# Attention and two gated MLPs on one core: Newton steps of two batches' roots moved to plain products, a gated tile kept in SBUF, planner constants set anew

## The chip, the cores and the metric

The kernel runs on one core of one Trainium2 chip. The metric is the device time in microseconds (us) of one execution. The engines are named as in the profile: PE is the matmul engine (PEld its weight loads), DVE the vector engine, ACT the scalar engine, POOL GpSimd, SP the engine whose queue issues most DMAs. Each engine runs its own instructions in order and waits on semaphores of the others.

## The reference, cut to what matters

Four batches, 12 heads, 448 positions, head size 64. Attention with root-mean-square normalised q and k feeds two gated MLPs in a row:

```python
rms = np.sqrt(np.mean(x * x, axis=-1, keepdims=True) + 1e-06)
q_n, k_n = q / rms_q * g_q, k / rms_k * g_k
attn = softmax(q_n @ k_n.T / 8);  x = attn @ v            # -> (4, 448, 768)
h = np.maximum(x @ moe_w_in, 0.0)                          # 768 -> 1024
x = (h * sigmoid(conv3(h))) @ moe_w_out                    # 1024 -> 768
out = (sigmoid(conv5(x)) * (x @ moe2_w_val)) @ moe2_w_out  # 768 -> 768
```

Inputs arrive as 64-bit floats; weights are converted on the chip and every operand is split into a high and a low fp16 part, so that a product is three fp16 matmuls.

## The kernel before, in words

**Stages.** A batch's attention is 21 units (three groups of four heads, seven units each: six of 128 query rows and one of remainders). A unit is: the score matmuls into a PSUM pair (`qk`), row maxima on DVE (`smax`, one `TENSOR_REDUCE ps<-ps 128x2` and a small product that goes to the tile `mx`), two exponentials on ACT (`sexp`), the split into fp16 parts `p`, a DMA transpose to `pt`, and the matmuls with the values (`av`). A batch's MLP has four stages, called w_in (8 tiles), w_out (6), w_val (6) and the output (7 half tiles). The attention of batch b+1 runs beside the MLP of batch b; the output of batch 0 is done late, after the w_in stage of batch 1. The MLP of batch 3 has nothing beside it.

**Roots.** Before a group of heads starts, `prep` squares and sums q and k and calls `rroot(x, y, t)`: an add, a shift and an integer step give a first guess of 1/sqrt(x), then three Newton steps refine it. `x` is the tile `ssq`, `y` one of three tiles `root`, `t` the tile `half`, 128 rows by 30 columns. A Newton step is three DVE instructions: `half<-root`, `half<-half,ssq`, `root<-half,root`, so nine in a root. The normalisation of k (`kin<-kin,root` on POOL) and the row maxima wait for it. There are twelve groups; the first is solved in three pieces.

**Gated tile.** In a w_in tile (`w_in_tile`) ACT writes relu(h) back into the PSUM bank `ps` and the middle tap to `scr`; DVE adds the two outer taps (`scr<-ps,cw,scr`); ACT takes tanh; `mul` multiplies into the PSUM bank; `hi` copies the high half to `act`; `lo` subtracts it (`act<-ps,act 128x448`) and closes the bank. `scr` has four buffers.

**Order.** All instructions are recorded with a wish time (`at`) and then put into an order by a planner (class `Plan`): it has estimated costs and picks, engine by engine, the ready instruction of highest priority. An instruction recorded through `vg` or `sub` may go to DVE or POOL, one through `copy` or `times` to DVE or ACT, whichever the planner expects to be done first; a lean (the constants `L_...`) is added to DVE's estimate. The add of log(4096) to `mx` in batches 2 and 3 is such a `vg`. Every instruction of the plan is emitted at line 378, so that is the line in all rows of the profile. What comes out is a fixed order per engine, with buffers and semaphores set at build time.

Of the kernel before, what the change touches and what calls it, by code (L numbers as in the profile page):

```python
# [25 lines left out]
class Plan:  # L26
# [355 lines left out]
def kernel(  # L382
# [172 lines left out]
    W_2 = 70.038  # L555
    W_2_STEP = 3.986
    RS_AT = -1.932
    RS_STEP = -0.224
# [15 lines left out]
    L_SQ = 2.046  # L574
    L_LOAD = 3.479
    L_WHI = 1.477
    L_WLO = 0.815
# [1064 lines left out]
```

## Time and profile before

| | us |
|---|---|
| median of 3 runs (651.45 to 652.5) | 651.65 |
| the profiled execution's own time | 651.15 |
| its span, first to last instruction | 649.4 |
| PE busy | 592.0 |
| DVE busy | 520.7 |
| ACT busy | 419.9 |
| POOL busy | 224.0 |

The shares are of a span with different stages. Attention of batch 0 fills the first 100 us; from there to about 253 us attention of batch 1 runs beside the MLP of batch 0; from about 253 to 420 us attention of batch 2 beside the MLP of batch 1; to about 551 us attention of batch 3 beside the MLP of batch 2; the rest is the MLP of batch 3. The rows below give busy times by these five stretches.

### The profile page before, as it was taken

Reading aid. Unit: us, or ns where it says so; the run is one execution under the profiler, and the core shown is the slowest. Engines: PE = TensorE matmul, PEld = TensorE weight load, DVE = VectorE, ACT = ScalarE, POOL = GpSimd, SP = SyncE. Lnnn points to the kernel's source line nnn. Section 1 sums busy time; section 2 is a strip of 40 time slices with the busy share of each in tenths; the row PEclk is TensorE's granted clock in tenths of the full one; section 3 lists DMA queues with packets and bytes.
Section 4 is the critical chain, followed back from the end, with each engine's and each line's share of the span. In section 5 each row is a group of like instructions: output and inputs, shape, how many; then the busy total and the mean of one; then the engine's idle time right before and its main releaser. Section 6 shows DMA issues by size and latency. Waiting matters only on the chain. (4 is left out here: it accounts for less than half of the span.)

```text
span 649.4 us, 12670 instructions
## 1 busy us (share of the span) xinstructions
PE 592.0 (91%) x4755; PEld 332.0 (51%) x4755; DVE 520.7 (80%) x1059; ACT 419.9 (65%) x735; POOL 224.0 (34%) x246
## 2 busy tenths in 40 slices
PE   4897899897996787999898999999999999999997
PEld 2665586453453344455454555555554565555554
DVE  6989799999999999999678885689997754498720
ACT  4787789878786876698557665578756455272211
POOL 2533465616325624545343442263444101000000
PEclk9988799897997989999999999999999999999999
DMA  8967667985987988993788587884646467200002
GB/s 207 230 141 182 137 127 213 205 204 103 189 165 175 229 169 157 191 204 104 163 165 155 106 141 150 169 166 85 102 90 108 86 124 146 47 0 1 2 13 74
DMA packets 254611, 88.06 MB, mean 136 GB/s; under 512 B 240671, under 2 KB 250453, under 8 KB 254549
## 3 DMA queue, kind: packets, MB, share of 16 engines
q1 hardware_dynamic: 254021, 87.12, 64.2%
q8 instruction: 37, 0.61, 0.4%
q14 instruction: 25, 0.20, 0.1%
q10 hardware_dynamic: 528, 0.13, 0.1%
HBM read 38.59 MB, written 5.51 MB: 68 GB/s over the span
## 5 line engine op out<-in xcount | busy, mean ns | idle before, releaser
L378 PE MATMUL ps<-act,wi 128*128 128x448 f16 x576 | 120.8, 359 | 4.6 <-DVE p L378 1.7
L378 PE MATMUL ps<-act,wo 128*128 128x448 f16 x576 | 122.1, 356 | 2.9 <-DVE act L378 2.6
L378 DVE TENSOR_REDUCE ps<-ps 128x2 f32<-128x896 f32 x84 | 91.2, 1093 | 18.6 <-PE ps L378 18.2
L378 ACT ACTIVATE p<-ps,mx,root 128x448 f32<-128x448 f32 x112 | 75.4, 722 | 41.6 <-POOL mx L378 31.6
L378 PE MATMUL ps<-act,wv 128*128 128x448 f16 x432 | 92.5, 358 | 8.1 <-DVE p L378 4.8
L378 PE MATMUL ps<-w,act 128*128 128x384 f16 (+1 forms) x576 | 93.3, 327 | 1.3 <-ACT osb L378 1.0
L378 PE MATMUL ps<-ka,qa 64*128 64x448 f16 (+3 forms) x560 | 80.9, 384 | 12.7 <-DVE p L378 5.6
L378 PEld LDWEIGHTS <-wi 128*128 128x128 f16 x576 | 55.3, 99 | 59.2 <-issue 14.7
L378 PEld LDWEIGHTS <-wo 128*128 128x128 f16 x576 | 54.9, 99 | 54.6 <-issue 11.2
L378 PE MATMUL ps<-vv,pt 128*128 128x65 f16 (+4 forms) x1488 | 79.8, 202 | 0.0
L378 ACT ACTIVATE act<-ps 128x448 f16<-128x448 f32 (+3 forms) x96 | 50.2, 531 | 44.4 <-PE ps L378 23.2
L378 PEld LDWEIGHTS <-pt 128*128 128x128 f16 (+1 forms) x1512 | 59.8, 101 | 25.3 <-issue 8.9
L378 POOL TENSOR_TENSOR p<-p,p 128x896 f16<-128x896 f32 x28 | 53.4, 1908 | 47.3 <-issue 27.6
L378 PEld LDWEIGHTS <-act 128*128 128x128 f16 (+1 forms) x576 | 48.7, 101 | 35.9 <-issue 8.0
L378 PEld LDWEIGHTS <-wv 128*128 128x128 f16 x432 | 41.1, 99 | 48.7 <-issue 15.2
L378 DVE SCALAR_TENSOR_TENSOR act<-ps,cw,act 128x444 f32<-128x444 f32 (+3 forms) x96 | 63.6, 676 | 0.8
L378 DVE SCALAR_TENSOR_TENSOR w<-w 128x768 uint32<-128x768 uint32 (+1 forms) x56 | 45.8, 826 | 1.6 <-POOL w L378 1.5
L378 PEld LDWEIGHTS <-qa 64*128 64x128 f16 (+1 forms) x528 | 21.8, 97 | 46.9 <-issue 32.7
L378 DVE SCALAR_TENSOR_TENSOR scr<-ps,cw,scr 128x447 f32<-128x447 f32 x64 | 41.8, 675 | 0.5 <-ACT scr L378 0.3
L378 ACT ACTIVATE p<-p 128x896 f16<-128x896 f32 x42 | 39.9, 950 | 0.4
L378 POOL TENSOR_SCALAR mx<-mx 128x2 f32<-128x2 f32 x37 | 9.1, 245 | 87.1 <-DVE mx L378 80.2
L378 POOL TENSOR_TENSOR kin<-kin,gb 112x512 f32<-112x512 f32 x22 | 29.9, 1363 | 17.6 <-ACT tk L378 13.2
(116 smaller groups left out, 920.1 us busy)
## 6 DMA issues: line engine op xcount, KB each, us to landing
w<-in_moe_w_in_dram SPq DMA_DIRECT2D x8, 768.0 KB, 5.2
w<-in_moe_w_out_dram SPq DMA_DIRECT2D x8, 768.0 KB, 5.4
kin<-in_k_dram SPq DMA_DIRECT2D x24, 224.0 KB, 3.6
act<-in_moe_w_out_dram SPq DMA_DIRECT2D x12, 384.0 KB, 4.0
w<-in_moe_w_val_dram SPq DMA_DIRECT2D x12, 384.0 KB, 4.2
out_dram<-osb SPq DMA_DIRECT2D x24, 192.0 KB, 2.2
qin<-in_q_dram SPq DMA_DIRECT2D x35, 128.0 KB, 3.2
vst<-in_v_dram SPq DMA_DIRECT2D x18, 224.0 KB, 3.6
```

What stands on the lines that cost most here:

```text
L378: getattr(getattr(nc, e), method)(*a, **k)
```

## The change

`rroot` gets a flag. With it, a Newton step is four plain instructions instead of three fused ones, each of which may go to DVE or POOL (`L_STEP` is negative, which favours DVE a little). It is set for batches 1 and 2 (`ROOTP_1`, `ROOTP_2`), which have three roots each. `LEAVE_IN` becomes one for batches 2 and 3: `mul` writes the gated tile into `scr`, the PSUM bank is closed there, `hi` reads SBUF and `lo` may go to POOL. A third option (`XSB`) is added and left at zero. About forty constants of the planner change a little.

```diff
     def rroot(x, y, t, pool):
         vg(L_ROOT, "tensor_scalar", x, x, D * 1e-6, None, ALU.add)
...
         for _ in range(3):
+            if pool:
+                vg(L_STEP, "tensor_tensor", t, y, y, ALU.mult)
+                vg(L_STEP, "tensor_tensor", t, t, x, ALU.mult)
+                vg(L_STEP, "tensor_scalar", t, t, -0.5, 1.5, ALU.mult, ALU.add)
+                vg(L_STEP, "tensor_tensor", y, y, t, ALU.mult)
+                continue
             nc.vector.scalar_tensor_tensor(t, y, -0.5, y, ALU.mult, ALU.mult)
             nc.vector.tensor_tensor(t, t, x, ALU.mult)
             nc.vector.scalar_tensor_tensor(y, t, 1.5, y, ALU.add, ALU.mult)
...
-            rroot(ss[:rows, c], rr[:rows, c], tmp[:rows, c])
+            rroot(ss[:rows, c], rr[:rows, c], tmp[:rows, c], ROOT_POOL[b] and not solo)
...
-    LEAVE_IN = (0, 0, 0, 0)
+    LEAVE_0 = 0
+    LEAVE_1 = 0
+    LEAVE_2 = 1
+    LEAVE_3 = 1
+    ROOTP_1 = 1
+    ROOTP_2 = 1
+    L_STEP = -0.143
...
-    L_ROOT = 0.504
+    L_ROOT = 0.445
-    SIGN_VAL = 2
+    SIGN_VAL = 3
-    VLEAD = 4.205
+    VLEAD = 5.845
```

The constants move nearly every instruction a little. Three places show what matters below.

**DVE, the third root of batch 1** (tiles `root_107` and `half_108`), beside the MLP of batch 0. `w_65` is a weight piece on its way to fp16, `cw_113` the taps of the second convolution, `rs` and `x` belong to the attention's output. Before:

```order
L378 SCALAR_TENSOR_TENSOR half_108<-root_107 128x30
L378 TENSOR_REDUCE ps<-ps 128x2
L378 TENSOR_TENSOR half_108<-half_108,ssq_104 128x30
L378 TENSOR_TENSOR x_0_80<-ps,x_0_80 128x384
L378 SCALAR_TENSOR_TENSOR root_107<-half_108,root_107 128x30
L378 SCALAR_TENSOR_TENSOR w_65<-w_65 128x384
L378 SCALAR_TENSOR_TENSOR half_108<-root_107 128x30
L378 SCALAR_TENSOR_TENSOR w_65<-w_65 128x384
L378 TENSOR_TENSOR half_108<-half_108,ssq_104 128x30
```

and now:

```order
L378 TENSOR_SCALAR root_107<-half_108 128x30
L378 SCALAR_TENSOR_TENSOR act<-ps,cw_113,act 128x444
L378 SCALAR_TENSOR_TENSOR p_1_91<-ps,p_1_91 128x896
L378 SCALAR_TENSOR_TENSOR act<-ps,cw_113,act 128x445
L378 TENSOR_TENSOR half_108<-root_107 128x30
L378 TENSOR_SCALAR w_65<-w_65 128x384
L378 SCALAR_TENSOR_TENSOR act<-ps,cw_113,act 128x446
L378 SCALAR_TENSOR_TENSOR w_65<-w_65 128x384
L378 TENSOR_SCALAR rs_109<-ps 128x6
```

Of this root DVE keeps the first guess and one product; the rest has left its queue.

**POOL, the same root.** `wv` is the low part of a weight of the w_val stage, `kin` the k rows that are normalised with the root. Before:

```order
L378 TENSOR_TENSOR wv<-w_65,wv 128x384 x3
L378 TENSOR_TENSOR w_65<-w_65,zero 128x384
L378 TENSOR_TENSOR wv<-w_65,wv 128x384
L378 TENSOR_TENSOR w_65<-w_65,zero 128x384
L378 TENSOR_TENSOR wv<-w_65,wv 128x384
L378 TENSOR_TENSOR kin_83<-kin_83,root_107 112x512
L378 TENSOR_TENSOR kin_84<-kin_84,root_107 112x512
L378 TENSOR_TENSOR wv<-w_65,wv 128x384
```

and now:

```order
L378 TENSOR_TENSOR half_108<-half_108,ssq_104 128x30
L378 TENSOR_TENSOR wv<-w_65,wv 128x384
L378 TENSOR_SCALAR half_108<-half_108 128x30
L378 TENSOR_TENSOR root_107<-root_107,half_108 128x30
L378 TENSOR_TENSOR half_108<-half_108,ssq_104 128x30
L378 TENSOR_SCALAR half_108<-half_108 128x30
L378 TENSOR_TENSOR root_107<-root_107,half_108 128x30
L378 TENSOR_TENSOR half_108<-root_107 128x30
L378 TENSOR_TENSOR half_108<-half_108,ssq_104 128x30
L378 TENSOR_SCALAR half_108<-half_108 128x30
L378 TENSOR_TENSOR w_65<-w_65,zero 128x384
L378 TENSOR_TENSOR root_107<-root_107,half_108 128x30
```

The chain of the root stands between the weights' low parts and ahead of the two normalisations, on one engine.

**POOL at its end, beside the last units of attention and in the MLP of batch 3.** Before:

```order
L378 TENSOR_SCALAR mx_102<-mx_102 128x2
L378 TENSOR_SCALAR mx_103<-mx_103 128x2
L378 TENSOR_SCALAR mx_100<-mx_100 128x2
L378 TENSOR_SCALAR mx_101<-mx_101 128x2
L378 TENSOR_TENSOR p_0_90<-p_0_88,p_0_90 128x896
L378 TENSOR_SCALAR mx_102<-mx_102 128x2
L378 TENSOR_SCALAR mx_103<-mx_103 128x2
```

and now:

```order
L378 TENSOR_SCALAR mx_102<-mx_102 128x2
L378 TENSOR_TENSOR p_0_90<-p_0_88,p_0_90 128x896
L378 TENSOR_TENSOR p_1_91<-p_1_89,p_1_91 128x896
L378 TENSOR_TENSOR act<-scr_95,act 128x448
L378 TENSOR_TENSOR act<-scr_96,act 128x448
L378 TENSOR_TENSOR act<-scr_97,act 128x448
L378 TENSOR_TENSOR act<-scr_94,act 128x448
L378 TENSOR_TENSOR act<-scr_95,act 128x448
```

Most adds to `mx` have gone from here to DVE, and low parts of the gated tile have come.

Counted over whole queues: of the 72 Newton instructions of the six roots (12 each) POOL gets 64 and DVE 8, where DVE had 54. Adds to `mx`: DVE 5 before and 23 now, POOL 37 and 19. Low parts of the gated tile in batches 2 and 3: DVE 16 before and 5 now, POOL none and 11. Counted on DVE up to its first tap of batch 1's first w_in tile (PE begins that stage in both orders after the same number of score and value matmuls): 537 instructions before, 487 now, and 45 row maxima ahead of it in both. Of the forms that differ there by more than 1 us, DVE has

| form on DVE, up to that tap | before | now |
|---|---|---|
| `half<-root`, `half<-half,ssq`, `root<-half,root` 128x30 (fused) | 18 of each | 6 of each |
| `scr<-ps,cw` 128x448 (middle tap, now mostly on ACT) | 5 | 1 |
| `act<-act` 128x384 (a weight piece's bits) | 12 | 10 |
| `tq<-qin` 128x896 (copy, now on ACT) | 4 | 2 |
| `w<-w` 128x384, TENSOR_SCALAR | 6 | 3 |
| `wo<-w,wo` 128x768 | 0 | 1 |

## Rows read from the trace of the kernel before

**Rows 1.** The profile page, part 1: busy us, share of span, instructions of each engine.

```profile
PE 592.0 (91%) x4755; PEld 332.0 (51%) x4755; DVE 520.7 (80%) x1059; ACT 419.9 (65%) x735; POOL 224.0 (34%) x246
```

**Rows 2.** Busy us (and instructions) by stretch: PE, PEld, DVE, ACT, POOL; PE clock; DMA.

```profile
0.00:100.00 100.00, 78.67 (x546) 56.14 (x547) 86.18 (x207) 75.03 (x133) 41.77 (x65) 0.93 0.75 175
100.00:253.00 153.00, 130.91 (x1109) 69.23 (x1107) 146.99 (x297) 121.87 (x218) 67.53 (x68) 0.93 0.83 179
253.00:420.00 167.00, 157.52 (x1373) 85.58 (x1373) 135.84 (x268) 111.41 (x197) 69.27 (x69) 1.00 0.77 155
420.00:551.00 131.00, 130.84 (x1169) 70.52 (x1168) 101.09 (x205) 81.81 (x134) 45.41 (x46) 1.00 0.62 112
551.00:649.40 98.40, 94.02 (x564) 50.55 (x562) 50.55 (x85) 29.75 (x57) 0.00 (x0) 0.99 0.09 25
```

**Rows 3.** Waits of PE, 100 to 253 us: us in total, times, longest.

```profile
PE ps L378 <- DVE p L378: 10.3, 4, 4.8
PE ps L378 <- DVE act L378: 6.2, 5, 2.3
...
PE ps L378 <- DVE x L378: 1.5, 2, 1.2
```

**Rows 4.** Timeline around PE's longest wait there: start, us, instruction, [idle before].

```profile
201.02 0.18 DVE L378 SCALAR_TENSOR_TENSOR root<-half,root 128x30 f32<-128x30 f32 x1
...
201.35 2.23 POOL L378 TENSOR_TENSOR kin<-kin,root 112x512 f32<-112x512 f32 x2 [0.50 <-DVE root L378]
...
203.54 0.91 POOL L378 TENSOR_TENSOR wv<-w,wv 128x384 f16<-128x384 f32 x1
...
204.49 2.40 PE L378 MATMUL ps<-act,wv 128*128 128x448 f16 x6 [4.76 <-DVE p L378]
```

**Rows 5.** DVE groups by form, whole span: busy us, mean ns, idle before.

```profile
L378 DVE SCALAR_TENSOR_TENSOR act<-act 128x384 uint32<-128x384 uint32 x24 | 17.0, 710 | 0.1
...
L378 DVE SCALAR_TENSOR_TENSOR half<-root 128x30 f32<-128x30 f32 x33 | 8.1, 246 | 0.2
L378 DVE TENSOR_TENSOR half<-half,ssq 128x30 f32<-128x30 f32 x33 | 7.4, 224 | 0.2
...
L378 DVE SCALAR_TENSOR_TENSOR root<-half,root 128x30 f32<-128x30 f32 x33 | 6.3, 192 | 0.3
...
L378 DVE TENSOR_SCALAR scr<-ps,cw 128x448 f32<-128x448 f32 x8 | 5.2, 673 | 7.0 <-ACT ps L378 7.0
...
L378 DVE TENSOR_SCALAR mx<-mx 128x2 f32<-128x2 f32 x5 | 3.8, 767 | 0.1
...
L378 DVE CAST tq<-qin 128x896 f16<-128x896 f32 x5 | 3.1, 622 | 0.0
...
L378 DVE TENSOR_SCALAR w<-w 128x384 uint32<-128x384 uint32 x6 | 2.0, 352 | 0.0
...
L378 DVE TENSOR_TENSOR wi<-w,wi 128x768 f16<-128x768 f32 x1 | 1.3, 1317 | 1.0 <-ACT wi L378 1.0
```

**Rows 6.** DVE's timeline in batch 1's third root: start, us.

```profile
195.66 0.19 DVE L378 TENSOR_TENSOR half<-half,ssq 128x30 f32<-128x30 f32 x1
195.76 0.56 DVE L378 TENSOR_TENSOR ps<-ps,rs 128x384 f32<-128x384 f32 x1
```

**Rows 7.** POOL groups by form, whole span: busy us, mean ns, idle before.

```profile
L378 POOL TENSOR_TENSOR p<-p,p 128x896 f16<-128x896 f32 x28 | 53.4, 1908 | 47.3 <-issue 27.6 <-ACT p L378 18.8 <-POOL p L378 0.3
...
L378 POOL TENSOR_TENSOR wv<-w,wv 128x384 f16<-128x384 f32 x12 | 10.9, 913 | 24.7 <-ACT wv L378 24.7
...
L378 POOL TENSOR_SCALAR mx<-mx 128x2 f32<-128x2 f32 x37 | 9.1, 245 | 87.1 <-DVE mx L378 80.2 <-DVE half L378 2.7 <-ACT scr L378 1.9
...
L378 POOL TENSOR_SCALAR ssq<-ssq 128x30 f32<-128x30 f32 x8 | 3.8, 476 | 3.9 <-DVE ssq L378 3.4
```

**Rows 8.** Timeline, DVE and POOL at once, in batch 0: start, us.

```profile
58.09 1.65 POOL L378 TENSOR_TENSOR wi<-w,wi 128x768 f16<-128x768 f32 x1 [3.03 <-ACT wi L378]
...
58.26 1.53 DVE L378 TENSOR_TENSOR half<-half,ssq 128x30 f32<-128x30 f32 x1
```

More of the change, by code (lines that the diff above doesn't have):

```diff
@@ L39 @@
     AHEAD = 42.251
-    URGENT = 0.604
+    URGENT = 0.596
     TICK = 10.24 / 3
@@ L46 @@
     PASSES = 4
-    MIX = 0.816
+    MIX = 0.818
     KEEP = 0.023
@@ L502 @@
     S_K1 = 10.211
-    S_DK = 1.001
-    S_LQ = 4.715
+    S_DK = 1.263
+    S_LQ = 4.632
     S_LK = -0.828
@@ L507 @@
     DT0 = 2.39
-    DT_1 = 5.035
-    DT_2 = 6.066
-    DT_3 = 6.124
+    DT_1 = 5.037
+    DT_2 = 6.044
+    DT_3 = 5.928
     LAG = 2
@@ L513 @@
     C_GATE = 2.001
-    C_MUL = 2.305
-    C_HI = 2.672
-    C_LO = 3.201
+    C_MUL = 2.338
+    C_HI = 2.578
+    C_LO = 3.244
     V_HI = 0.203
-    A_HI = 0.828
+    A_HI = 1.222
     A_LO = 1.33
@@ L521 @@
     E_PTR = 0.777
-    E_AV = 2.092
-    X_LAG = 2.123
+    E_AV = 2.342
+    X_LAG = 2.135
     MPE = 97.144
@@ L526 @@
     M_1 = -6.504
-    M_2 = -5.288
+    M_2 = -5.351
     M_3 = 5.405
@@ L530 @@
     APART = 2.77
-    L_TAP = -0.251
+    L_TAP = -0.285
     LATE = 1
@@ L548 @@
     QD_ = 1.286
-    W_IN = -80.001
+    W_IN = -79.489
     W_IN_STEP = 0.794
-    W_OUT = -18.15
+    W_OUT = -19.05
     W_OUT_STEP = 1.022
@@ L554 @@
     W_VAL_STEP = 0.65
[L555 to L558, printed above, removed]
+    W_2 = 69.947
+    W_2_STEP = 3.814
+    RS_AT = -1.836
+    RS_STEP = -0.209
     BIG_IN = 1
@@ L571 @@
     WIDE_2 = 1
[L574 to L577, printed above, removed]
-    L_ROOT = 0.504
+    L_SQ = 3.972
+    L_LOAD = 3.334
+    L_WHI = 2.364
+    L_WLO = 1.037
+    L_ROOT = 0.445
     L_QHI = -0.391
@@ L582 @@
     L_NORM = 4.697
-    L_KHI = 1.117
-    L_KLO = 0.737
-    L_GLO = -0.143
+    L_KHI = 1.865
+    L_KLO = 0.781
+    L_GLO = 0.326
     L_MUL = 1.103
     MUL = 0.0
-    LEAVE_IN = (0, 0, 0, 0)
-    L_PLO = 0.577
+    LEAVE_0 = 0
+    LEAVE_1 = 0
+    LEAVE_2 = 1
+    LEAVE_3 = 1
+    XSB_1 = 0
+    XSB_2 = 0
+    XSB_3 = 0
+    ROOTP_0 = 0
+    ROOTP_1 = 1
+    ROOTP_2 = 1
+    ROOTP_3 = 0
+    L_XLO = 0.9
+    L_STEP = -0.143
+    L_PLO = 0.668
     L_VM = -0.571
-    L_VHI = 1.353
-    L_VLO = 1.574
-    L_PHI = 2.165
+    L_VHI = 1.418
+    L_VLO = 1.46
+    L_PHI = 2.172
     L_PT = 5.435
@@ L600 @@
     WIDE = [(0, r) for r, w in enumerate((WIDE_0, WIDE_1, WIDE_2)) if w]
+    LEAVE_IN = (LEAVE_0, LEAVE_1, LEAVE_2, LEAVE_3)
+    X_SBUF = (0, XSB_1, XSB_2, XSB_3)
+    ROOT_POOL = (ROOTP_0, ROOTP_1, ROOTP_2, ROOTP_3)
     FLAT = [(0, r) for r, f in enumerate((FLAT_0, FLAT_1, FLAT_2)) if f]
@@ L1183, with x_split @@
     x_there = set()
-    def x_split(dst, src):
+    def x_split(dst, src, sbuf=False):
         copy(L_XHI, dst[:, 0], src)
-        nc.vector.tensor_tensor(dst[:, 1], src, dst[:, 0], ALU.subtract)
+        if sbuf:
+            sub(L_XLO, dst[:, 1], src, dst[:, 0])
+        else:
+            nc.vector.tensor_tensor(dst[:, 1], src, dst[:, 0], ALU.subtract)
     def x_pair(b, j):
@@ L1207, in x_pair @@
         o = nxt(x16, "x16")
-        x32 = x_scaled(wide, xp, FULL, r)
-        x_split(o.rearrange("p a c (h d) -> p a c h d", h=2), x32)
-        close_bank(xp)
+        x32 = x_scaled(wide, xp, FULL, r, nxt(scr, "scr")[:, 0 : FULL * P] if X_SBUF[b] else None)
+        if X_SBUF[b]:
+            close_bank(xp)
+        x_split(o.rearrange("p a c (h d) -> p a c h d", h=2), x32, X_SBUF[b])
+        if not X_SBUF[b]:
+            close_bank(xp)
         dst = xslot(b, j)
@@ L1235, in x_rem @@
         o = xr16[0]
-        x32 = x_scaled(wide, u.xp, 1, rr)
-        x_split(o.rearrange("p a (c h d) -> p a c h d", c=1, h=2), x32)
-        close_bank(u.xp)
+        x32 = x_scaled(wide, u.xp, 1, rr, nxt(scr, "scr")[:, 0:P] if X_SBUF[b] else None)
+        if X_SBUF[b]:
+            close_bank(u.xp)
+        x_split(o.rearrange("p a (c h d) -> p a c h d", c=1, h=2), x32, X_SBUF[b])
+        if not X_SBUF[b]:
+            close_bank(u.xp)
         for i in range(2):
```

2 lines of the change are left out of this document (1 added, 1 removed).

## The prediction

> **What bounds the kernel now.** Part 1 of the page gives PE 91% of the span, DVE 80% and POOL 34% [rows 1], means over stages with different limits, so I read the five stretches next [rows 2]. Until 100 us PE idles 21 us, from 100 to 253 us 22.1 (153 less 130.9), from 253 to 420 us 9.5, and from there to 551 us nothing (131 less 130.8); the MLP of batch 3 alone is dense but for its start and end. So the kernel has two halves. After 253 us PE is the bound, and its work is the same before and after the change. Before that, something starves PE, at a clock of 0.93, a mix of its two levels, where it is 1.00 later. Between 100 and 253 us it is DVE: it is busy 147.0 of 153 us, ACT 121.9, POOL 67.5 [rows 2]. The waits say so too: of PE's 22.1 us, 18.0 ended with a DVE instruction (10.3 + 6.2 + 1.5) [rows 3]. The longest, 4.76 us, is put down to DVE, but PE starts at 204.49, when POOL's low part of a w_val weight has just ended (203.54 + 0.91), and that stood on POOL behind two normalisations which had waited for the last step of a root on DVE [rows 4]. A root late on DVE thus holds POOL, and through POOL the weights.
>
> PE needs every microsecond that it gets after 253 us, so a microsecond that DVE's queue loses ahead of batch 1's w_in stage is worth up to one at the end, and one that it loses later is worth nothing.
>
> **DVE's queue ahead of batch 1's w_in stage.** The counts are those of the table in the section on the change, the durations those of [rows 5]. The fused Newton steps: 12 fewer of each of three forms, 12 x (0.246 + 0.224 + 0.192) = -7.9 us. Middle taps that ACT now does: -4 x 0.673 = -2.7. Weight bits: -2 x 0.710 and -3 x 0.352 = -2.5. Copies of q: -2 x 0.622 = -1.2. One low part of a weight comes to DVE, priced by its like for w_in: +1.3. Together -13.0. But a row's duration is more than it takes from the queue: at 195.66 a step of 0.19 us is followed by the next instruction after 0.10 [rows 6]. Taking 0.09 off each of the 46 instructions that these forms lose in net gives back 4.1: -8.9. The other forms differ by one or two instructions each and nearly cancel; in net four fewer, which at 0.56 us, like the product of [rows 6], would be -2, and since they are mixed I take half: -1.1. Sum: **-10.0 us**; the ends are -15 (no overlap) and -8.9.
>
> **POOL's side of it.** Four roots stand ahead of that place (three of batch 1, the first of batch 2): 12 instructions each, of which DVE keeps two, so 46 on POOL. No row shows a 30-column product there. The nearest are 0.913 us at 384 and 1.908 at 896 columns [rows 7], which is 1.94 ns a column and 0.17 us fixed, so 0.23 at 30 columns; the scale-and-add of that shape is 0.476 (`ssq`) [rows 7]. 34 x 0.23 + 12 x 0.476 = 13.5 us, into a stretch where POOL idles more than half the time. A chain of twelve takes 9 x 0.23 + 3 x 0.476 = 3.5 us if nothing comes between, where the nine steps on DVE, spread among other work, ended at 201.2 after starting before 195.66 [rows 4, 6]. So the normalisation should not come later than now.
>
> POOL's work can hold DVE, however. At 58.26 the product `half<-half,ssq` took 1.53 us while POOL worked on a weight from 58.09 to 59.74 [rows 8]; the same product takes 0.19 at 195.66 [rows 6]. The mean of its 33 rows is 0.224 [rows 5], so such holds are rare or short. Charged to DVE are between 0 and all 13.5 us; I take a tenth, +1.3, nearer to the mean than to the single row.
>
> The page SBUF — State Buffer of the Trainium skill, section Who interferes with whom, says that the pair of ports shared by the two engines is an exclusive lock, which holds a DVE instruction with two SBUF inputs for the whole of a GpSimd instruction that reads SBUF. The row at 58.26 agrees with it, the mean of the 33 rows shows how seldom it bites. By the rule alone each microsecond moved to POOL could come back on DVE, which is the third rival below.
>
> New waits: DVE idles 6.0 us of its 153 [rows 2]. A queue that is shorter by 10 will wait more often for PE and ACT, which do not get less work. Between 0 and all 10 us; I take a quarter of what it idles now, +1.5.
>
> **After 253 us.** Adds to `mx`: 18 more on DVE, 10 of them ahead of batch 2's w_in stage. On DVE one takes 0.767 us [rows 5], on POOL 0.245 [rows 7]: 13.8 us more on DVE, in two stretches where it idles 31.2 and 29.9 [rows 2]. That idle time is the cover; without it the price is paid in full. Each add lies between row maximum and exponential, 0.52 us slower than on POOL, and two units are always in flight. Taken at 0; the ends are 0 and 18 x 0.522 = +9.4. Gated tile: 16 products are as long as before, 11 low parts go from DVE to POOL (128x448, between 0.23 and 1.908 us there by [rows 7]), and banks come free one copy and one subtraction earlier. PE does not idle from 420 to 551 us, and in the last stretch 4.4 us, start and end of the kernel included [rows 2], so nothing is to be gained; `scr`, now held until the low part is done, has four buffers, more than the two tiles in flight. Taken at 0. The two roots of batch 2 that lie after 253 us, and the three more weight pieces whose sign is masked on POOL, lie under the same idle time of DVE and POOL: 0. PE's 9.5 us of idle time there could shrink by perhaps half as DVE's queue arrives earlier: -4 at the lower end.
>
> **Sum.** -10.0 + 1.3 + 1.5 = -7.2 against the profiled execution's own 651.15 us: 643.95. The median of the runs shown is 0.5 above that execution, so I forecast **644.4 us** for a median.
>
> **The rivals.**
> First, more than that: with PE less starved the granted clock between 100 and 253 us rises from 0.93 towards 1.00. Seven hundredths of 153 us is 10.7 us at most; half of it gives 644.4 - 5.3 = 639.1. For it: the clock is 1.00 in the two stretches in which PE idles least [rows 2]. Against it: PE still idles over 10 us there.
>
> Second, no change: the gain is reached at 253 us and given back between 253 and 551 us, because the adds to `mx` on DVE hold up the exponentials: -7.2 + 7 to 9.4 gives 651.4 to 653.8, mostly within 0.2% of now. For it: 0.767 us for two columns [rows 5] says that such an instruction is often held. Against it: more than 60 us of DVE's idle time.
>
> Third, slower: the lock. If POOL's whole 13.5 us are charged to DVE, -10.0 + 13.5 + 1.5 = +5.0 gives 656.6. It decides from the point at which 8.5 of the 13.5 us, six tenths, are charged. The single row [rows 8] speaks for it, the mean [rows 5] against it. It is what the page on SBUF would make of this change.
>
> Fourth, slower: POOL late with the weights of the w_val stage. PE has already waited 4.76 us for one [rows 4], and the third root now stands among the low parts of `wv`, 3.5 us of chain, with three more masked pieces of about 0.913 each [rows 7]. Two such waits more on PE, each with half of the masked pieces (1.4 us), 2 x (3.5 + 1.4) = 9.8, turn -7.2 into +2.6: 654.2 by the profiled run, 654.7 as a median. It decides where PE reaches a w_val matmul before POOL has left the chain. Against it: PE has more w_out work ahead of its first w_val matmul than before.
>
> That the change does not do what it says is excluded by the order: 64 of 72 Newton instructions are on POOL.
>
> **How the numbers follow.** Forecast 0.52, clock 0.12, given back 0.13, lock 0.12, weights 0.11. A measurement of this kernel tells about 0.2% (1.3 us) from no change. Faster by more than that: 0.52 + 0.12 = 0.64; within: 0.13; slower: 0.12 + 0.11 = 0.23. The forecast's own range is 639 (no overlap between instructions, nothing lost) to 649 (half of the gain lost to waits). To hold 8 in 10 the range takes in the case without change, half of the clock's case and of that of the weights, and leaves out the lock: **637.5 to 654.5**.
>
> **What would show it.** Right: batch 1's w_in stage, which now begins at the end of the second stretch, 253 us [rows 2], begins 6 to 9 us earlier; DVE's busy time up to there is shorter; PE's waits for DVE up to 253 us fall by about as much as the total; the stretches after it are as long as now. Clock: PE's clock up to that place is above 0.95. Lock: the mean durations of DVE's products and copies from SBUF rise, and the stage begins no earlier. Weights: a wait of PE of 3 us or more at a w_val matmul of batch 0 that ends with a POOL instruction. Given back: PE idles more than 15 us from there to the last score matmul. The forecast is wrong above all if DVE waits more than I allow, that is if ACT or the DMA transposes come next after it by less than 10 us.

## The result

| | before | changed |
|---|---|---|
| median of 4 runs each, same chip (us) | 651.58 (651.45 to 652.5) | 643.2 (641.82 to 643.75) |
| ratio, 95% interval | | 0.9865 (0.9847 to 0.9884) |
| the profiled execution's own time, its span | 651.15, 649.4 | 643.0, 641.2 |

The changed kernel is faster by 8.4 us; the forecast was 7.2 us, 644.4. On three other chips the kernel before had medians of 656.6 to 657.7 and single runs from 650.7 to 662.2, while the changed kernel, run again on one of them, stayed at 643.66, a ratio of 0.9789. Each experiment below is therefore set against the runs of the kernel before on its own chip. The longer an execution of the kernel before, the lower, by and large, PE's mean clock in it: on one of these chips the shortest, 650.71, had 0.971 and the longest, 661.49, had 0.956 (last section). Lowest against lowest, the changed kernel gains 9.7 us on its second chip (642.6 and 652.32).

### The profile page after: what moved, and what is told of

It reads as the page before. It is cut to its first block, busy times and chain, and to the rows that moved or that the text cites. A ratio compares the mean times of both kernels' runs of the same rounds, so it can differ in the third digit from the quotient of the medians.

```text
span 641.2 us, 12698 instructions
## 1 busy us (share of the span) xinstructions
PE 591.9 (92%) x4755; PEld 334.8 (52%) x4755; DVE 510.4 (80%) x1011; ACT 419.6 (65%) x739; POOL 254.5 (40%) x308
## 4 chain that ended last, share of the span: by engine, by line
PE 57%; DVE 24%; DMA 8%; ACT 5%; issue 3%; SPq 2%; ACTq 0%; DVEq 0%
PE ps L378 57%; DVE ps L378 6%; DVE act L378 6%; DVE w L378 4%; DVE scr L378 3%; DVE p L378 2%; DMA w<-in_moe_w_val_dram 2%; SPq L378 2%; DMA act<-in_moe_w_out_dram 2%; DMA pt<-p 2%; DVE ssq L378 1%; ACT p L378 1%; DMA w<-in_moe_w_in_dram 1%; ACT act L378 1%; ACT w L378 1%
## 5 line engine op out<-in xcount | busy, mean ns | idle before, releaser
L378 PE MATMUL ps<-act,wo 128*128 128x448 f16 x576 | 123.6, 361 | 1.3 <-DVE act L378 0.8
L378 PE MATMUL ps<-act,wv 128*128 128x448 f16 x432 | 89.8, 353 | 1.5 <-ACT wv L378 1.1
L378 PE MATMUL ps<-vv,pt 128*128 128x65 f16 (+3 forms) x1488 | 88.2, 204 | 0.0
L378 PEld LDWEIGHTS <-wi 128*128 128x128 f16 x576 | 55.3, 100 | 61.7 <-issue 18.7
L378 PEld LDWEIGHTS <-pt 128*128 128x128 f16 (+1 forms) x1512 | 63.6, 101 | 26.5 <-issue 8.3
L378 ACT ACTIVATE act<-ps 128x448 f16<-128x448 f32 (+4 forms) x81 | 43.0, 536 | 49.2 <-PE ps L378 25.6
L378 DVE SCALAR_TENSOR_TENSOR act<-ps,cw,act 128x446 f32<-128x446 f32 (+3 forms) x96 | 63.6, 676 | 0.9
L378 PE MATMUL ps<-vm,pt 128*128 128x130 f16 (+3 forms) x248 | 29.3, 234 | 5.0 <-DMA pt<-p 3.5
```

What stands on the lines that cost most here:

```text
L378: getattr(getattr(nc, e), method)(*a, **k)
```

## The profile after

Part 1 of the page, which answers [rows 1]: DVE has lost 10.3 us and POOL has gained 30.5; its Newton steps take 20.3 (below), its eleven low parts of the gated tile 11.3.

```profile
PE 591.9 (92%) x4755; PEld 334.8 (52%) x4755; DVE 510.4 (80%) x1011; ACT 419.6 (65%) x739; POOL 254.5 (40%) x308
```

The prediction spoke of what happens up to batch 1's w_in stage. So here the span is cut where the w_in stages of batches 0 to 3 begin (by PE's timeline), not at the fixed times of [rows 2]. The columns are those of [rows 2]: PE, PEld, DVE, ACT, POOL; PE clock; DMA. The kernel before:

```profile
0.00:117.29 117.29, 93.34 (x666) 66.22 (x667) 103.05 (x240) 91.41 (x160) 53.65 (x81) 0.94 0.75 178
117.29:253.99 136.70, 116.24 (x988) 59.15 (x988) 131.12 (x265) 106.49 (x192) 55.65 (x52) 0.93 0.84 178
253.99:417.44 163.45, 155.93 (x1365) 84.79 (x1365) 132.98 (x264) 108.64 (x192) 68.28 (x67) 1.00 0.78 157
417.44:547.34 129.90, 128.77 (x1157) 69.38 (x1156) 100.75 (x202) 83.02 (x136) 46.40 (x48) 1.00 0.60 110
547.34:649.40 102.06, 97.68 (x583) 52.48 (x582) 52.76 (x91) 30.31 (x59) 0.00 (x0) 0.99 0.13 30
```

The changed kernel, cut at the same places of the program:

```profile
0.00:113.57 113.57, 93.50 (x666) 67.78 (x667) 99.78 (x226) 91.84 (x162) 55.72 (x93) 0.90 0.79 181
113.57:244.98 131.41, 115.23 (x989) 59.43 (x989) 124.47 (x234) 108.68 (x199) 68.26 (x89) 0.94 0.88 184
244.98:410.27 165.29, 159.87 (x1371) 86.66 (x1371) 132.99 (x259) 108.04 (x191) 78.49 (x82) 0.97 0.75 154
410.27:538.45 128.18, 124.85 (x1109) 67.63 (x1108) 102.94 (x208) 81.13 (x134) 44.80 (x39) 1.00 0.62 115
538.45:641.20 102.75, 98.47 (x625) 53.29 (x624) 50.28 (x86) 29.87 (x57) 7.22 (x7) 1.00 0.13 30
```

Up to batch 1's w_in stage DVE was busy 103.05 + 131.12 = 234.2 us and is now busy 99.78 + 124.47 = 224.25: 9.9 us less. The stage begins at 244.98, 9.0 us earlier. PE does the same work there (208.7 us now, 209.6 before) and idles 8.2 us less (36.25, before 44.4). The next stretch is 1.8 us longer than before, the one after it 1.7 shorter, the last 0.7 longer: -9.0 + 1.8 - 1.7 + 0.7 = -8.2, the difference of the spans. The last two stretches don't hold the same work in both kernels: by the records 48 matmuls fewer now lie in the fourth and 42 more in the fifth.

The 9.0 us have two parts. The first root whose Newton steps leave DVE is batch 1's first. The integer step of its first guess, right ahead of them, ends on DVE at 89.41 before and at 86.19 now. So 3.2 us of the 9.0 lie ahead of that place, and 5.8 between it and the w_in stage (164.58 us before, 158.79 now). The experiments below use the same place.

PE's waits between 100 and 253 us, beside [rows 3]:

```profile
PE ps L378 <- DVE p L378: 9.3, 6, 4.2
PE ps L378 <- DVE act L378: 5.7, 4, 3.4
PE ps L378 <- DVE scr L378: 1.8, 2, 1.0
PE ps L378 <- ACT wv L378: 1.1, 2, 0.8
PE ps L378 <- ACT act L378: 0.4, 1, 0.4
PE ps L378 <- POOL wv L378: 0.3, 1, 0.3
```

DVE still ends most of them, 16.8 us where it was 18.0; the wait of 3.4 at the start of batch 1's w_in stage, which now lies at 245, is counted here and was not before. Cut by stage, from batch 0's w_in stage up to and with the wait at the start of batch 1's, they fell from 18.5 to 14.3 us. Ahead of it they didn't fall (8.8 and 9.4); there it is the waits for ACT's `p` that did, from 10.8 to 7.0. No w_val matmul waits 4.76 us as in [rows 4] any more: ACT's and POOL's `wv` hold PE for 1.1 + 0.3 us. But PE's longest wait is hardly shorter: 4.21 us before a score matmul at 198.31, ended by DVE's `p`.

The third root of batch 1 on POOL's timeline, where [rows 4] showed its last step on DVE at 201.02 and the normalisation at 201.35 (start, us):

```profile
180.30 0.23 POOL L378 TENSOR_TENSOR half<-root 128x30 f32<-128x30 f32 x1 [1.55 <-DVE root L378]
180.61 0.25 POOL L378 TENSOR_TENSOR half<-half,ssq 128x30 f32<-128x30 f32 x1
...
184.37 0.22 POOL L378 TENSOR_SCALAR half<-half 128x30 f32<-128x30 f32 x1
186.15 0.83 POOL L378 TENSOR_TENSOR w<-w,zero 128x384 f32<-128x384 f32 x1 [1.56 <-ACT w L378]
186.94 0.26 POOL L378 TENSOR_TENSOR root<-root,half 128x30 f32<-128x30 f32 x1
187.27 2.05 POOL L378 TENSOR_TENSOR kin<-kin,root 112x512 f32<-112x512 f32 x2
```

The chain takes 7.0 us from its first product on POOL to the start of the normalisation, not 3.5. Ahead of its last product stands a weight product, for which POOL waits 1.56 us on ACT and then works 0.83. Still the normalisation comes 14 us earlier, 10.9 of them counted from the place named above. Of POOL's groups by form, the Newton steps and the adds to `mx` (busy us, mean ns | idle before), beside [rows 7]:

```profile
L378 POOL TENSOR_TENSOR half<-root 128x30 f32<-128x30 f32 x16 | 7.1, 443 | 11.1 <-DVE root L378 10.5
L378 POOL TENSOR_TENSOR half<-half,ssq 128x30 f32<-128x30 f32 x16 | 4.9, 305 | 2.1 <-DVE half L378 1.1
L378 POOL TENSOR_SCALAR mx<-mx 128x2 f32<-128x2 f32 x19 | 4.7, 249 | 41.1 <-DVE mx L378 40.2 <-DVE rs L378 0.2
L378 POOL TENSOR_SCALAR half<-half 128x30 f32<-128x30 f32 x16 | 4.3, 268 | 1.2
L378 POOL TENSOR_TENSOR root<-root,half 128x30 f32<-128x30 f32 x16 | 4.0, 248 | 1.7 <-DVE half L378 0.6
```

Of DVE's groups, beside [rows 5]:

```profile
L378 DVE TENSOR_SCALAR mx<-mx 128x2 f32<-128x2 f32 x23 | 11.1, 487 | 0.6
...
L378 DVE TENSOR_TENSOR half<-half,ssq 128x30 f32<-128x30 f32 x17 | 3.1, 185 | 0.2
```

## The experiments

Theory: what counts is DVE's queue ahead of batch 1's w_in stage, and the roots are the main part of what left it. Rivals: the roots don't matter and the new order does it; the port shared by DVE and POOL, or the adds to `mx`, eat part of the gain; the parts pay alone in any order.

Where nothing else is said, the planner's order was frozen: every engine keeps the order of the kernel named, and only the instructions in question are put on another engine, or have one added behind or ahead of them, as they are emitted (the diffs are shortened; a name like `root_step[i]` marks these). Ratios are to the kernel before on the same chip, with 95% intervals. This table, from PE's timeline of one execution of each, is used throughout: the time to the start of batch 0's w_in stage, the stretches from one w_in stage to the next, and from the last to PE's last matmul (us). An execution in the table need not be a median one: that of before_roots_pool is the shortest of its twelve, that of load_early the shortest of its five, that of load_late the longest of its ten. The first column differs by 7.8 us between before and load_late, which have one order up to there, so what an edit does is read behind the place where it begins.

| kernel | to w_in 0 | 0 to 1 | 1 to 2 | 2 to 3 | 3 to end |
|---|---|---|---|---|---|
| before | 117.3 | 136.7 | 163.5 | 129.9 | 97.7 |
| changed | 113.6 | 131.4 | 165.3 | 128.2 | 98.5 |
| after_again | 113.2 | 132.8 | 164.9 | 127.8 | 98.5 |
| roots_dve | 113.8 | 137.4 | 167.1 | 127.5 | 98.7 |
| before_roots_pool | 113.6 | 137.2 | 165.5 | 130.2 | 97.8 |
| pool_doubled | 110.8 | 133.8 | 164.6 | 127.5 | 98.5 |
| mx_pool | 110.4 | 132.9 | 165.8 | 128.3 | 98.6 |
| load_early | 117.6 | 147.8 | 162.0 | 129.9 | 97.7 |
| load_late | 125.1 | 137.3 | 168.8 | 130.6 | 98.4 |
| constants_only | 117.3 | 135.1 | 166.1 | 128.7 | 98.8 |
| no_rootp | 117.1 | 137.1 | 166.0 | 127.8 | 98.7 |
| flags_only | 122.7 | 137.3 | 167.5 | 133.1 | 97.5 |
| batch0_roots_pool | 108.6 | 132.5 | 166.4 | 127.8 | 98.6 |
| glo_dve | 111.0 | 133.2 | 165.5 | 130.2 | 100.3 |

From the integer step of batch 1's first root to batch 1's w_in stage (us; in load_late and glo_dve nothing is edited up to there, so they are further executions of the two orders; the four kernels in the old order reach the step between 86.0 and 96.4, with nothing edited ahead of it):

| kernel | that step ends at | from there to w_in 1 | DVE busy in it |
|---|---|---|---|
| before | 89.4 | 164.6 | 158.5 |
| load_late | 96.4 | 166.0 | 159.1 |
| before_roots_pool | 86.0 | 164.7 | 155.3 |
| load_early | 89.8 | 175.6 | 171.7 |
| changed | 86.2 | 158.8 | 151.2 |
| after_again | 85.8 | 160.2 | 151.4 |
| glo_dve | 84.2 | 160.1 | 151.4 |
| pool_doubled | 84.0 | 160.5 | 153.1 |
| roots_dve | 85.1 | 166.1 | 158.1 |

### The roots' steps back on DVE, in the new order

```diff
             _, method, a, k = self.ops[i][0][e]
+            if root_step[i]: e = "vector"
             getattr(getattr(nc, e), method)(*a, **k)
```

> The changed kernel in its own order, with the 64 Newton products that GpSimd does put on DVE at the same places of the order. My theory (a microsecond in DVE's queue ahead of batch 1's w_in stage is one at the end, and the roots carry about half of the gain): 46 more instructions on DVE ahead of that stage at 0.10 to 0.13 us each, so 4 to 6 us slower than the changed kernel, 647 to 649.5 us; w_in of batch 1 begins at 249 to 251 us. Rival (the gain comes from the new order and the other moved forms, the roots are too short to matter): under 1.5 us slower, 643 to 644.7.

Measured: 652.71 us, ratio 0.9939 (0.9908 to 0.9971). That is 9.5 us above the changed kernel's 643.2 (from another chip; on this one pool_doubled, in the same order, had 643.18), and 7.6 us by the spans of the profiled executions (648.8 and 641.2). The stretch from batch 0's to batch 1's w_in stage:

```profile
113.77:251.17 137.40, 114.98 (x989) 59.38 (x989) 130.93 (x268) 108.85 (x199) 58.69 (x55) 0.95 0.85 178
```

DVE is busy 6.5 us more there than in the changed kernel (130.93 and 124.47), and the stretch is 6.0 us longer (137.4 and 131.4; 4.2 to 4.6 against glo_dve and after_again), at PE's same work. From the first root on it is 166.1 us against 158.8 to 160.2. So the roots' steps on DVE cost there about what they take of its queue, and the rival that they don't matter is out. These are twelve plain steps in a root where the kernel before has nine fused ones, so they put back more than was there; no_rootp below has the fused ones. The next stretch adds 1.8 us, and the whole is more than the theory's range.

### The roots' steps on POOL, in the old order

The twelve plain products take the place of the nine fused steps of all roots of batches 1 and 2; nothing else changes.

```diff
-            nc.vector.scalar_tensor_tensor(t, y, -0.5, y, ALU.mult, ALU.mult)
-            nc.vector.tensor_tensor(t, t, x, ALU.mult)
-            nc.vector.scalar_tensor_tensor(y, t, 1.5, y, ALU.add, ALU.mult)
+            nc.gpsimd.tensor_tensor(t, y, y, ALU.mult)
+            nc.gpsimd.tensor_tensor(t, t, x, ALU.mult)
+            nc.gpsimd.tensor_scalar(t, t, -0.5, 1.5, ALU.mult, ALU.add)
+            nc.gpsimd.tensor_tensor(y, y, t, ALU.mult)
```

> The kernel before in its own order, with the fused Newton steps of batches 1 and 2 replaced, at the same places, by plain products on GpSimd. My theory: DVE loses 36 instructions ahead of batch 1's w_in stage at 0.10 to 0.15 us of queue each, 3.6 to 5.4 us, and the end comes 3 to 5 us earlier, 646.5 to 648.5 us. Rival (the port that the two engines share makes DVE wait for each of GpSimd's products, or the chain comes late for the normalisation of k): no gain, 651 us or more.

Measured: 655.65 us, ratio 0.9979 (0.9947 to 1.0011): a gain isn't shown. The first three stretches:

```profile
0.00:113.55 113.55, 92.19 (x667) 65.82 (x667) 100.60 (x231) 91.38 (x160) 59.19 (x93) 0.94 0.79 183
113.55:250.74 137.19, 116.65 (x987) 59.30 (x987) 129.49 (x238) 106.54 (x191) 65.06 (x88) 0.91 0.84 178
250.74:416.28 165.54, 157.56 (x1365) 85.46 (x1365) 131.26 (x246) 108.76 (x192) 74.68 (x91) 0.99 0.77 155
```

Up to batch 1's w_in stage DVE is busy 100.60 + 129.49 = 230.1 us, 4.1 less than before, 3.2 of them behind the first edited step. The stage begins at 250.74 where it began at 253.99, but that lead is not the edit's: this execution was 3.4 us ahead when it reached the first edited step (86.0 and 89.4), and from there the way to the stage is as long as before:

```profile
89.41:253.99 164.58, 140.98 (x1197) 77.47 (x1198) 158.48 (x323) 131.27 (x234) 71.12 (x73) 0.94 0.84 180
86.01:250.74 164.73, 141.12 (x1196) 77.60 (x1197) 155.33 (x286) 131.08 (x233) 86.21 (x118) 0.93 0.83 179
```

The first line is the kernel before. DVE is busy 3.2 us less there (158.48 and 155.33), and PE gains nothing by it (at most 1.3 us, against load_late's 166.0). My theory fell here, and the rival's time came, but the port alone is not the reason, since DVE's busy time did fall. The third root's normalisation begins 112.4 us behind the first edited step, where it began 111.9 behind it (in the changed kernel 101.1), and PE's longest wait, that of [rows 4], stands as it was: 4.90 us ahead of a w_val matmul at 200.76. So in the old order the steps went to POOL without the root being done sooner. That this is why nothing was gained is likely, not shown. The next stretch is 2.1 us longer, 1.6 of it in PE's busy time (157.56, before 155.93) at a clock of 0.99, not 1.00.

### Twice the work on POOL

Behind each of the 64 steps on POOL a like one on a spare tile (behind a scale-and-add a scale-and-add), in the changed kernel's order.

```diff
             getattr(getattr(nc, e), method)(*a, **k)
+            if root_step[i] and e == "gpsimd":
+                nc.gpsimd.tensor_tensor(spare2, spare, spare, ALU.mult)
```

> The changed kernel with each Newton product on GpSimd followed by a like one on a spare tile, which nobody reads: twice the work of the roots on GpSimd, nothing more on DVE. My theory (GpSimd has room, and a tenth of what it does is charged to DVE): 0.5 to 2.5 us slower, 643.7 to 645.7 us. Rival (lock of the shared port: all of it is charged): 46 more of 0.23 to 0.48 us ahead of batch 1's w_in stage, 10 us or more, so at least 6 us slower, 649 or more.

Measured: 643.18 us (640.77 to 648.44), ratio 0.9812 (0.9766 to 0.9859), the changed kernel's own time. The added steps took 13.5 + 3.5 = 17.0 us of POOL:

```profile
L386 POOL TENSOR_TENSOR spare<-spare 128x30 f32<-128x30 f32 x48 | 13.5, 281 | 0.0
...
L384 POOL TENSOR_SCALAR spare<-spare 128x30 f32<-128x30 f32 x16 | 3.5, 220 | 0.0
```

From batch 0's to batch 1's w_in stage DVE's busy time is 126.77 us, 2.3 more than in the changed kernel, for 6 us more on POOL (74.24 and 68.26):

```profile
110.78:244.56 133.78, 116.22 (x989) 59.60 (x989) 126.77 (x235) 109.58 (x199) 74.24 (x123) 0.93 0.89 183
```

So less than four tenths of POOL's added time came back on DVE there, and nothing that can be seen at the end. The rival of the lock, 6 us or more, is out for these steps.

### All adds to `mx` on POOL

```diff
             _, method, a, k = self.ops[i][0][e]
+            if mx_add[i]: e = "gpsimd"
             getattr(getattr(nc, e), method)(*a, **k)
```

> The changed kernel in its own order with all 23 adds to the row maxima that DVE does put on GpSimd. My theory (they lie under DVE's idle time in the stretches in which PE is the bound): within 1 us of the changed kernel, 642 to 644.5 us. Rival (part of the gain is given back after 253 us because these adds hold up the exponentials): 3 us faster or more, 640 or less.

Measured: 645.47 us, ratio 0.9823 (0.9784 to 0.9862), a little above the theory's range and not faster than the changed kernel, whose 23 adds on DVE take 11.1 us. In the stretch behind batch 1's w_in stage DVE is busy 5.4 us less (127.55 and 132.99) and the stretch is no shorter (165.8 and 165.3). Nothing was being given back there.

### A load on DVE, early and late

In the kernel before, in its order, a copy of 448 columns from PSUM to a spare tile ahead of the row maxima of 18 units, once of batch 1 (early), once of batch 2 (late).

```diff
             _, method, a, k = self.ops[i][0][e]
+            if row_maximum_of_unit_2_to_19[i]:
+                nc.vector.tensor_copy(spare, ps[:, 0, 0:448])
             getattr(getattr(nc, e), method)(*a, **k)
```

> The kernel before in its own order, with 18 copies from PSUM to a spare tile added on DVE (448 columns, 0.62 us each, some 0.53 us of queue), one ahead of the row maxima of units 3 to 20 of batch 1's attention, so all but a few of them ahead of batch 1's w_in stage: 9.5 us of queue. My theory (there DVE is the bound): the end comes 7 to 10 us later than before, ratio 1.011 to 1.015. Rival (DVE is busy there, but what ends last is something else): under 4 us, ratio under 1.006.

Measured: 667.38 us, ratio 1.0168 (1.0132 to 1.0205), some 11 us, a little above the theory's range. The copies, and the stretch in which they lie:

```profile
L381 DVE CAST spare<-ps 128x448 f16<-128x448 f32 x18 | 11.0, 613 | 0.7 <-PE ps L382 0.7
```

```profile
117.64:265.45 147.81, 120.19 (x987) 60.71 (x987) 144.47 (x283) 107.03 (x192) 55.52 (x52) 0.88 0.80 165
```

Less 0.09 us of overlap each the copies take 9.4 us of the queue. DVE's busy time grew by more, 13.4 us; the weights' bit products (`w<-w` 128x384) are 2.8 us longer by their records. The stretch is 11.1 us longer (147.81, before 136.70). PE idles 27.6 us, 7.2 more, and the rest, 4.0 us, is in its busy time, for a matmul fewer by the records, at a clock of 0.88 where it was 0.93: in this execution the starved PE lost a second time. By the spans 9.9 us of it reach the end (659.3 and 649.4).

> The same 18 copies, ahead of the row maxima of units 3 to 20 of batch 2's attention, where I hold PE to be the bound and DVE to have 31 us to spare. My theory: 0 to 3 us later than before, ratio 1.000 to 1.005. Rival (DVE bounds in both halves): 7 to 10 us, ratio 1.011 to 1.015.

Measured: 663.86 us, ratio 1.0089 (1.0046 to 1.0132), some 6 us (3 to 9), above the theory's range and below the rival's. The profiled execution lost time in its first 125 us, ahead of the copies, and only the stretch with them is read:

```profile
262.38:431.15 168.77, 158.19 (x1366) 85.51 (x1365) 142.01 (x282) 108.92 (x192) 68.55 (x67) 0.99 0.78 151
```

It is 5.3 us longer than before (168.77 and 163.45), though DVE had 30 us of idle time there; PE idles 3.1 us more and is busy 2.3 longer, at a clock of 0.99 where it was 1.00. So a microsecond added on DVE costs after 253 us something like half of what it costs ahead of it, not nothing. The copies stand between a unit's scores and its row maxima, so they delay the unit as well as fill the queue; which of the two costs was not told apart.

### The parts one by one, each in an order of its own

Here the planner made the order anew. First the new constants alone, both options off:

```diff
-    LEAVE_2 = 1
-    LEAVE_3 = 1
-    ROOTP_1 = 1
-    ROOTP_2 = 1
+    LEAVE_2 = 0
+    LEAVE_3 = 0
+    ROOTP_1 = 0
+    ROOTP_2 = 0
```

> The changed kernel's constants with both options off (roots in fused steps on DVE, gated tile in PSUM), ordered anew by the planner. My theory (the roots off DVE's queue carry at least half of the gain): 4 us or more slower than the changed kernel, ratio to the kernel before 0.992 to 1.000. Rival (the new constants carry the gain): ratio 0.985 to 0.989, like the changed kernel.

Measured: 653.85 us, ratio 0.9918 (0.9887 to 0.9949). The changed kernel ran beside it:

> The changed kernel once more, on the chip of the other runs of this call, as their reference. Every theory: 0.985 to 0.988 of the kernel before.

Measured: 643.66 us, ratio 0.9789 (0.9761 to 0.9818), below what was expected, because the kernel before was longer on this chip (657.69, where it was 651.58). So some 4 to 5 us come with the constants, and 10 us more with the options.

The constants and the gated tile, without the roots:

```diff
-    ROOTP_1 = 1
-    ROOTP_2 = 1
+    ROOTP_1 = 0
+    ROOTP_2 = 0
```

> The changed kernel with the roots of batches 1 and 2 left in fused steps on DVE, ordered anew; constants and the gated tile in SBUF as changed. My theory (the roots off DVE's queue are the larger half of the gain): 4 to 7 us slower than the changed kernel, 647.5 to 650.5 us; the stretch from batch 0's to batch 1's w_in stage is 3 us longer or more. Rival (gated tile and constants carry the gain): within 2 us of the changed kernel.

Measured: 652.67 us, ratio 0.9941 (0.9902 to 0.998): no better than the constants alone, within the intervals, and slower than the theory's range. So the 9 to 10 us belong to the roots in an order made with them, as in roots_dve; in the table the two kernels without them need 2 to 6 us more from w_in 0 to w_in 1. They also reach w_in 0 some 4 us later, but that column differs as much between executions of one order.

Both options with all the old constants:

```diff
-    L_ROOT = 0.445
+    L_ROOT = 0.504
-    SIGN_VAL = 3
+    SIGN_VAL = 2
-    VLEAD = 5.845
+    VLEAD = 4.205
...
```

> Both options of the change with the constants of the kernel before, ordered anew. My theory: the roots' share comes without new constants too, 4 to 6 us faster than before, 645.5 to 648 us, ratio 0.990 to 0.994. Rival (the options pay only in an order that was made for them): ratio 0.997 or more.

Measured: 662.11 us, ratio 1.0097 (1.0049 to 1.0145): slower than before. My theory fell here too. The rival holds, that the options pay only in an order made for them. The first stretch and the fourth are longer than before (122.7 and 133.1), the first at a clock of 0.85. In the fourth, where I had said that nothing could be lost, PE is busy 130.9 of 133.1 us:

```profile
427.43:560.51 133.08, 130.90 (x1158) 69.84 (x1156) 102.03 (x199) 80.86 (x134) 51.91 (x52) 1.00 0.56 108
```

Before it was 128.77 of 129.90, for one matmul fewer by the records; where these 2.1 us of PE come from I did not resolve.

### The low parts of the gated tile back on DVE

```diff
             _, method, a, k = self.ops[i][0][e]
+            if gated_low_part[i]: e = "vector"
             getattr(getattr(nc, e), method)(*a, **k)
```

> The changed kernel in its own order with the 11 low parts of the gated tile that GpSimd does put on DVE. My theory (they lie where PE is the bound): within 1 us of the changed kernel, 642 to 644.5 us. Rival (the gated tile on GpSimd carries part of the gain): 2 us slower or more.

Measured: 646.16 us, ratio 0.9871 (0.9812 to 0.9931); that is 2.5 to 3 us above the changed kernel on the other chips (643.2 and 643.66), and 5 above batch0_roots_pool on the same one. The last two stretches:

```profile
409.76:540.00 130.24, 125.68 (x1109) 67.79 (x1108) 104.49 (x212) 81.58 (x134) 40.81 (x35) 1.00 0.61 113
540.00:644.60 104.60, 99.11 (x625) 53.24 (x624) 53.72 (x93) 30.36 (x57) 0.00 (x0) 1.00 0.13 29
```

Both grew, by 2.1 and 1.85 us (130.24 and 128.18, 104.60 and 102.75), where DVE took over POOL's eleven subtractions, 630 ns each. PE idles 2.4 us more in the two together. The six other executions of that order with these subtractions on POOL lie between 127.5 and 128.3, and between 98.5 and 98.7 where this one has 100.3 (table), so the difference is clear of their spread. The theory fell and the rival was right: in the changed order their place matters, though no_rootp shows no gain of the option as a whole over constants_only.

### Batch 0's second and third root on POOL as well

The same four plain instructions as above, now also for the two roots of batch 0 that are solved whole, in the changed kernel's order.

```diff
-            rroot(..., ROOT_POOL[b] and not solo)
+            rroot(..., ROOT_POOL[b] and not solo, on_pool=b == 0 and not solo)
```

> The changed kernel in its own order, with the steps of the second and third root of batch 0 on GpSimd as plain products too. My theory (DVE bounds the first stretch as well): 18 steps of 0.10 to 0.15 us less on DVE, 0.5 to 2.5 us faster than the changed kernel, 641 to 643 us. Rival (GpSimd brings the w_in weights' low parts late there): slower than the changed kernel by 1 us or more.

Measured: 641.12 us (640.24 to 643.32), ratio 0.9791 (0.974 to 0.9842). That is 2 to 2.5 us below the changed kernel's medians on other chips, as expected, but the ratio to the kernel before is after_again's own (0.9789), and the lowest runs of the two are near each other (640.24 and 641.82): a gain over the changed kernel isn't shown. What the profiled execution gains lies in the first stretch (108.6; the changed order otherwise 110.4 to 113.8), whose clock was 0.97, where in the others it was 0.90 to 0.94.

## Why the prediction was right, and where it was off

**The two halves.** Right ahead of 253 us for the changed order: putting the roots back on DVE (roots_dve) and adding to its queue (load_early) each moved batch 1's w_in stage by about the same amount. Not right for the old order: there 3.2 us taken off DVE's queue (before_roots_pool) moved nothing. "Worth up to one" is reached only where the order lets the root, and what waits for it, come sooner. Off behind 253 us as well: "one that it loses later is worth nothing" held for the adds to `mx`, where 5.4 us off DVE gained nothing (mx_pool), but not the other way round: load_late shows about a half, and glo_dve 2.5 to 3 us for eleven subtractions. The step of the prediction that failed there read DVE's idle time of [rows 2] as cover. My reading is that DVE idles there because a unit's steps wait on each other, so that a longer step in that chain delays PE all the same; that was not shown by itself.

**DVE's queue, -10.0.** Together with the lock's +1.3, which a busy time holds too, that is -8.7; measured are -9.9, 7.3 of them behind the first moved step. Of its terms only the roots were measured alone, in the old order: -3.2 against the 4.7 that 7.9 less 36 x 0.09 for overlap makes (before_roots_pool). That the others make up the rest is counted from the order, not shown. The stage begins 9.0 us earlier, where 7.2 follow from the sum and 6 to 9 were given. But 3.2 of the 9.0 lie ahead of the first moved step, where executions of one order differ by more than that; that the total came within about a microsecond is in part luck. The forecast's own range begins at 639, which is -13.0 without overlap; the sum's own lower end, -15, would have made it 637.

**POOL's steps.** Products were priced at 0.23 us and scale-and-adds at 0.476; their means are 0.25 to 0.44 and 0.268. All 64 take 20.3 us, for which the estimates give 48 x 0.23 + 16 x 0.476 = 18.7. Two errors of opposite sign nearly cancelled. The chain of a root took 7.0 us where 3.5 was worked out for the case that nothing comes between; other work came between.

**The lock, +1.3.** It was over-feared as a rival. 17 us more of small instructions on POOL cost nothing that can be seen at the end. The prediction's sign, longer means on DVE, is mixed: `half<-half,ssq`, 0.224 us before, is 0.185 now, but the weights' TENSOR_SCALAR `act<-act` 128x384 rose from 0.391 to 0.623. It is 0.610 in roots_dve too, so it is not the roots' steps on POOL that lengthen it. The page SBUF — State Buffer of the Trainium skill calls the shared pair, in Who interferes with whom, an exclusive lock. That is not contradicted: pool_doubled's 2.3 us more on DVE would fit it. That these 2.3 us are the lock is not shown.

**New waits, +1.5.** The term is what DVE idles more. Up to batch 1's w_in stage it idled 19.8 us before and 20.7 now, 0.9 more: that is what separates the 9.9 us off its queue from the 9.0 by which the stage moved. The sign that PE's waits for DVE fall by about as much as the total came by less than half: 3.6 us of the 8.2 that PE idles less (18.5 and 8.8 together before, 14.3 and 9.4 now); most of the rest, 3.8 us, are waits for ACT's `p` in the first stretch, which the prediction did not have.

**After 253 us, 0.** The sum of the three stretches is +0.8 us (+1.8 - 1.7 + 0.7), so 0 was about right, though not for the reason given. The adds to `mx` cost 0.487 us, not 0.767, and no gain is seen from taking them off (mx_pool). "The stretches after it are as long as now" held to within 2 us, the last two with matmuls moved from one to the other. In the stretch after batch 1's w_in stage PE's busy time grew by 3.9 us (its clock is 0.97 there, not 1.00, and the records hold six matmuls more), while its idle time shrank from 7.5 to 5.4.

**The rivals.** The clock did not rise: 0.90 and 0.94 in the first two stretches, where it was 0.94 and 0.93. Weights hardly held PE (1.1 and 0.3 us), so POOL was not late. Its price had a slip: -7.2 + 9.8 on 651.15 is 653.75 by the profiled run and 654.2 as a median, not 654.2 and 654.7. Giving back is out for the adds to `mx`.

**What the sum hid.** The terms were added as though each were worth its price alone. The runs say otherwise: constants alone -4 to -5 us, options alone +5 to +6, both together -8 on the first chip and -14 on a later one, where the kernel before was longer. The prediction counted instructions in the final order, ahead of one stage; counted by parts it would have failed.

**Open.** Why the old constants make the options lose; why relief gains nothing in the old order; how much of the 3.2 us ahead of the first moved step is the change; and whether the changed order has fewer long executions. The changed kernel's eight runs lie between 641.8 and 645.2, but pool_doubled, in its order, reached 648.44.

## What to carry to other kernels

Find the place where the bound passes from one engine to another, count what the starved engine's supplier has in its queue ahead of that place in the old and the new order, and price the difference by the trace with the overlap taken off; here that gave the shift of the stage to two microseconds and the total to one, with some luck. A shorter queue is worth nothing by itself: ask whether the step that the bound engine waits for comes sooner in the new order. And before an edit is given a lead, see that the two executions were level where the edit begins. An engine's idle time is no cover for a step that stands in a chain which the bound engine waits for: ask where in the chain the step stands, not how busy the engine is. In a kernel ordered by a planner the parts of a change do not add up, so judge a move of work between engines together with the order that was made for it.

## What the runs showed of the hardware

The first stretch depends on when PE's clock comes back. Kernels in the changed order reached batch 0's w_in stage at 110.4 to 113.8 us, and in the two compared here the difference lies in a spell at half clock (0.50, that is 1.2 of 2.4 GHz). The changed kernel, from 40 to 68 us:

```profile
40.00:44.00 4.00, 2.12 (x17) 1.71 (x16) 3.93 (x10) 2.85 (x6) 0.50 (x1) 1.00 0.62 133
44.00:48.00 4.00, 4.00 (x21) 3.34 (x23) 2.85 (x5) 3.01 (x8) 1.64 (x1) 0.52 1.07 212
...
56.00:60.00 4.00, 4.00 (x18) 3.20 (x17) 3.46 (x10) 2.71 (x6) 1.65 (x1) 0.50 0.58 194
60.00:64.00 4.00, 4.00 (x22) 3.77 (x23) 1.86 (x7) 1.88 (x3) 2.64 (x2) 0.50 0.60 196
64.00:68.00 4.00, 4.00 (x33) 2.70 (x34) 1.82 (x4) 3.92 (x7) 1.10 (x1) 0.92 0.00 1
```

and pool_doubled, whose first added step comes later, in the last three of these:

```profile
56.00:60.00 4.00, 4.00 (x19) 3.04 (x17) 3.45 (x9) 2.71 (x6) 1.64 (x1) 0.52 0.68 198
60.00:64.00 4.00, 4.00 (x38) 3.42 (x37) 3.04 (x9) 3.83 (x7) 2.65 (x2) 1.00 0.60 189
64.00:68.00 4.00, 4.00 (x38) 2.99 (x36) 2.35 (x8) 3.98 (x8) 2.16 (x2) 1.00 0.09 22
```

In the changed kernel PE had idled 1.9 of 4 us before the clock fell, and in both kernels it was busy throughout from 56 us on. In pool_doubled the clock was back at 60 us, in the changed kernel not until after 64: 38 matmuls against 22 in the four microseconds between. So two executions of one order can differ by some 3 us here. In the old order it is more. load_late is the kernel before up to batch 2, and with the same 666 matmuls it took 125.1 us to batch 0's w_in stage where the kernel before took 117.3:

```profile
0.00:125.10 125.10, 99.78 (x666) 70.86 (x667) 104.04 (x240) 91.43 (x160) 55.11 (x81) 0.88 0.73 166
```

Of the 7.8 us, 6.4 are PE's busy time (99.78 and 93.34); its clock is 0.88 where it was 0.94, and 0.50 from 40 to 48 us, where the kernel before has 1.00. That is more than most of the edits above move. Whether the other long executions of the kernel before lose their time in the same place isn't shown; their mean clocks fit it. load_early showed the same price in another place: PE's busy time grew by 4.0 us at unchanged work when its clock fell from 0.93 to 0.88.
